# Maxima of two heads as 64-row products side by side, their unread result in PSUM, and the dense branch's output kept in the keys' room

## The chip, the cores and the metric

The kernel runs on one core of a Trainium2 chip. A core has a matrix engine (TensorE, PE in the profile, its weight loads on a row of their own, PEld), a vector engine (VectorE, DVE), a scalar engine (ScalarE, ACT), a general engine (GpSimd, POOL) and a sync engine (SyncE, SP) which here issues all DMAs, in order, from one queue. Operands lie in SBUF (128 partitions), results of TensorE in PSUM (eight banks of 2 KB per partition), inputs, outputs and scratch in HBM. The metric is the device time of one execution in microseconds.

## The reference, cut to what matters

```python
def reference(A_x, A_wqkv, A_wo, B_x, B_w1, B_b1, B_w2, B_b2, gate_w):   # S 2048, D 512, H 32, Dh 16, W 256, F 1792
    x = A_x
    g = sigmoid((x * gate_w).sum(-1, keepdims=True))
    q, k, v = heads(x @ wqkv)                       # 32 heads of 16
    scores = einsum("bhqd,bhkd->bhqk", q, k) * Dh ** -0.5
    scores = where(0 <= q_idx - k_idx < 256, scores, -1e9)
    a = heads_joined(softmax(scores) @ v) @ wo
    b = gelu(x @ w1 + b1) @ w2 + b2                 # dense branch, tanh form
    return g * a + (1 - g) * b
```

All is float32. Every query sees itself and the 255 positions before it.

## The kernel before, in words

**Precision.** Each float32 operand of a dense product is split into a high part rounded to TensorE's fast 32-bit format and the rest; `mm3` (L88 to L92) adds three products, so a dense step is three 128x512 matmuls of lines L90, L91 and L92.

**Two streams.** The generator `dense` yields dense work in such steps: `qkv` (projections, tiles `qk`, `v`), `mlp` (tiles `u`, then `y`, in two halves of the hidden width; `TURNS` gives the order of half and chunk of 512 rows), then `final` (tiles `a`, the output projection and the mix with the gate). Beside it runs attention, in units of one group of four heads (`g_`) and one block of 128 rows: 8 groups of 16 blocks, 128 units. A unit has four iterations; each does, in the order of `ORDER`, one maxima product (`att_max`, tile `sm`, L394), one scores product (`att_exp`, tile `st`, L435) for a unit eight units earlier (`LEAD`), and a filling of dense steps. The maxima are needed first because the row maximum is subtracted inside the scores product.

**Maxima.** `att_max` multiplies queries by keys, 128 queries against up to 384 keys, over 96 contraction rows: `qs[0:96]` and `ks[0:96]` hold the high and low parts of the queries and keys of two heads (of a pair `pr`); the two heads `s` of a pair share the rows, told apart by the columns of `ks` (`of_head`), where the other head's rows hold zeros. VectorE then adds the mask and takes the row maximum (L399), and writes the masked scores, which nobody reads, to a bfloat16 tile `jm` in SBUF. Line L399 is there twice: the pass over the scores, and a read of the accumulator into `M`. `sm` has three PSUM banks.

**Rows.** After four blocks `att_rows` negates and transposes the maxima, and GpSimd writes them to `qs[96:104]` (L419). `ks[96:104]` holds ones at the own head (`own`).

**Scores and values.** The scores product goes over all 128 rows; ScalarE exponentiates into `pt` (L450), GpSimd cuts the mask's triangles (L441, L444). Every fourth unit `att_pvs` multiplies `pt` by the values: matmuls of 64 rows by 32 columns with an explicit position in the array (`tile_position=(r, 32 * i)`, L476), eight positions, the two row halves into two PSUM banks (`pv_st`, `pv_sm`). All other matmuls take the array whole. These float32 products stand in the trace as two matmuls each.

**Loads of a chunk.** `att_load` fetches for a group and a chunk of 512 rows the keys (`load_k`) and the queries (L372, L373) from HBM scratch, one chunk per four units.

**The end.** Dense results of the two halves go to HBM (`YA`, `YB`); `final` reads back `YB` (`load_y`, L681), scales it by 1 - g on ScalarE (`scale_y`, L687, in place) and adds it (L716). Attention's results pass through HBM for the division (`att_norm`: `ND`, `RD`, `OT`) and come back in `load_o` (L561, tiles `or`, `ot`).

**What sets the order.** The order on each engine is written out by a small planner: `tick` advances a clock by the planned time of TensorE's work, `after(ns, ...)` puts the work of other engines on a list at a time of that clock, and each engine's queue gets its instructions in that order. `need` forces listed work forward. `GELU` holds the delays of the six steps of the activation function.

Of the kernel before, what the change touches and what calls it, by code (L numbers as in the profile page):

```python
# [18 lines left out]
T = 512  # L19
# [13 lines left out]
def gated_mix(ctx: ExitStack, tc: tile.TileContext, x, wqkv, wo, w1, b1, w2, b2, gate_w, out):  # L33
# [11 lines left out]
    def f32(ap):  # L45
        return ap.bitcast(F32)
# [3 lines left out]


    SQ = [dr.tile([H, 16, 2, T], F32, name=f"SQ{t}") for t in range(NT)]
    SK = dr.tile([H, 16, 2, S], F32, name="SK")
    SV = [dr.tile([T, H, 17], F32, name=f"SV{t}") for t in range(NT)]
    XT = [dr.tile([NC, 128, 2, T], F32, name=f"XT{t}") for t in range(NT)]
# [22 lines left out]
    for k in (0, 1):  # L78
        nc.gpsimd.affine_select(out=own[96:104], in_=own[96:104], pattern=[[-2, 4]], compare_op=ALU.not_equal,
                                fill=1.0, base=-k, channel_multiplier=1)  # L80
    nms = cp.tile([128, RB, 32], F32R, name="nm")
    nc.gpsimd.memset(f32(nms), 0.0)
    vbuf = cp.tile([128, 2, NB * 68 + 16], F32, name="vbuf")
# [76 lines left out]
    def load_now(key):  # L160
        load_raw(key)
        after(LAND, split, key, nc.vector)

# [184 lines left out]
    def load_k(g_, c, prs):  # L348


        need(("qk", c, NC + g_ // 2))
        for pr in range(prs.start, prs.stop):
            for s in range(2):
                src = SK[4 * g_ + 2 * pr + s]
                for r, n, part in ((32 * s, 32, src.rearrange("d u c -> (d u) c")), (64 + 16 * s, 16, src[:, 0])):
                    v = f32(ks[r:r + n, pr])
                    k0, m = (c * T, NB) if s == 0 else (c * T - 64, NB) if c else (64, NB - 1)
                    to = v[:, 2 * k0 + 64:2 * k0 + 64 + 256 * m] if s else v[:, 2 * k0:2 * k0 + 256 * m]
                    to = to.rearrange("r (n x) -> r n x", x=256)
                    to = to[:, :, 0:128] if s else to[:, :, 64:192]  # L360
                    nc.sync.dma_start(to, part[:, k0:k0 + 128 * m].rearrange("r (n x) -> r n x", x=128))
                    if s and c == 0:
                        nc.sync.dma_start(v[:, 0:64], part[:, 0:64])
                    if s and c == NT - 1:
                        nc.sync.dma_start(v[:, 2 * S - 64:2 * S], part[:, S - 64:S])

    def att_load(g_, c, q_only=False):
        need(("qk", c, g_ // 2))
        if not q_only:
            load_k(g_, c, slice(0, 2))  # L370
        src, to = SQ[c][4 * g_:4 * g_ + 4], f32(qs[:, :, c * T:(c + 1) * T])
        nc.sync.dma_start(to[0:64], src.rearrange("(a s) d u c -> (s d u) a c", a=2))  # L372
        nc.sync.dma_start(to[64:96], src[:, :, 1].rearrange("(a s) d c -> (s d) a c", a=2))  # L373

    def att_load_v(g_, c):
        need(*[("v", c, b) for b in range(NB)])
# [8 lines left out]
    def att_max(g_, b, i):  # L385

        if b % RB == 0 and (g_, b // RB) not in Ms:
            Ms[g_, b // RB] = sb.tile([128, RB, 4], F32, tag="M", bufs=2, name=f"M{g_}_{b}")
        M = Ms[g_, b // RB]
        k0 = max(b - 2, 0) * 128  # L390
        w = (b + 1) * 128 - k0
        pr, s = divmod(i, 2)
        p = ps.tile([128, 384], F32, tag="sm", bufs=3, name=f"sm{g_}_{b}_{i}")
        nc.tensor.matmul(p[:, :w], qs[0:96, pr, b * 128:(b + 1) * 128], of_head(ks[0:96, pr, 2 * k0:2 * (k0 + w)], s),  # L394
                         start=True, stop=True)
        junk = sb.tile([128, 384], BF16, tag="jm", bufs=1, name=f"jm{g_}_{b}_{i}")

        def red():
            nc.vector.tensor_tensor_reduce(junk[:, :w], p[:, :w], mask[:, 384 - w:384], 1.0, -3e38,  # L399
                                           ALU.add, ALU.max, M[:, b % RB, i:i + 1])  # L400
            done.add(("max", g_, b, i))
        tick(w / 2.4 + 13)
        after(100, red)

    def att_rows(g_, rb):
# [198 lines left out]
    def ya_load(k):  # L604
# [7 lines left out]
        else:  # L612
            need(("y", 0, t, b))
            nc.sync.dma_start(ya, YA[t][slice(b * 128, (b + 1) * 128)])

    def mlp(n):
        half, t = TURNS[n]
        if n == 0:
# [24 lines left out]
        def y_start(b):  # L643
            if n + 1 == len(TURNS) and b == 2:
                load_o(0)
            if n + 1 == len(TURNS) and b == 3:
                load_y(0)
            ps_[b] = ps.tile([128, D], F32, tag="d", bufs=2, name=f"y{t}_{half}{b}")

        def y_end(b):  # L650
            ts = slice(b * 128, (b + 1) * 128)
            y = sb.tile([128, D], F32, tag="sq", bufs=2, name=f"yo{t}_{half}{b}")
            nc.vector.scalar_tensor_tensor(y, ps_[b], 0.5, yas.pop(n * NB + b), op0=ALU.mult, op1=ALU.add)
            ya_load(n * NB + b + 2)
            nc.sync.dma_start((YA, YB)[half][t][ts], y)
            done.add(("y", half, t, b))


# [12 lines left out]
            if i == HF - 1:  # L671
                after(100, y_end, b)

    ybs = {}

    def load_y(t):

        need(*[("y", 1, t, b) for b in range(NB)])
        for i in range(NB // 2):
            v = f32(sb.tile([128, 2, T], F32R, tag="w", bufs=14, name=f"yb{t}_{i}"))  # L680
            nc.sync.dma_start(v, YB[t].rearrange("(i j p) f -> i p j f", j=2, p=128)[i])  # L681
            for j in range(2):
                ybs[t * NB + 2 * i + j] = v[:, j]

    def scale_y(nb):

        nc.scalar.activation(ybs[nb], ybs[nb], AF.Copy, scale=g1[:, nb:nb + 1])  # L687
        done.add(("yb", nb))

    def final(t):  # L690
        ot = xts["o", t]
        if t < NT - 1:
            load_o(t + 1, range(NC) if t < NT - 2 else range(NC - 1))
        for i in ((1, 2), (3,), (), ())[t]:
            load_y(i)
        for b in range(NB):
            ts = slice(b * 128, (b + 1) * 128)
            nb = t * NB + b
            if t == NT - 2 and b == 2:
                load_o(t + 1, range(NC - 1, NC))  # L700
            after(YLAND if nb == 0 else 0, scale_y, nb)
            a = sb.tile([128, 2, 320], F32, tag="pt", bufs=PTS, name=f"ao{nb}")
            a = a.rearrange("p a b -> p (a b)")[:, 0:D]
            n = LASTN if nb == NT * NB - 1 else 1
            for k in range(n):
                cs = slice(k * D // n, (k + 1) * D // n)
# [6 lines left out]

                def ev(p=p, nb=nb, a=a, cs=cs):
                    need(("yb", nb))
                    nc.vector.scalar_tensor_tensor(a[:, cs], p, g[:, nb:nb + 1], ybs[nb][:, cs],  # L716
                                                   op0=ALU.mult, op1=ALU.add)
                    nc.sync.dma_start(out[nb * 128:(nb + 1) * 128, cs], a[:, cs])
                after(100, ev)
# [35 lines left out]
    for u in range(-LEAD, NU):  # L755
# [26 lines left out]
MM3 = 3 * 227  # L782
LPOS = 0
LASTN = 2
YLAND = 3200
WARM = (7, 3)
RB = 4
NKB = S // 128
# [37 lines left out]
```

## Time and profile before

| | us |
| --- | --- |
| median of three runs | 776.58 (775.4 to 778.53) |
| the profiled execution | 779.54 |
| its span, first to last instruction | 777.6 |
| PE busy | 751.4 |
| DVE busy | 533.4 |
| ACT busy | 432.8 |
| POOL busy | 384.9 |

The mean granted TensorE clock was 0.993. A matmul's duration in the profile includes its way through the array, and its end is modelled; how long a matmul holds the array is read from the distance of two starts. A timeline row gives start, duration, engine, line, operation, tiles, shapes and, in brackets, the idle time before it. A "x2" at the end of such a row merges two instructions.

### The profile page before, as it was taken

The page shows a single profiled execution, that of the slowest core. Times are in us where ns is not written, and L with a number is a line of the kernel's source. Part 1 is how long each engine was busy: PE and PEld are TensorE (multiplying, and loading weights), DVE is VectorE, ACT ScalarE, POOL GpSimd, SP SyncE. Part 2 cuts the span into 40 slices and gives each one's busy share as a digit, 9 for nine tenths or more (in the row PEclk, how much of TensorE's full clock was granted, in tenths as well). Part 3 has the DMA queues.
Part 4 walks back from the last instruction along what each step waited for, and adds up shares of the span by engine and source line. Part 5 has one row for each costly group of instructions (what it writes and reads, how often), then busy time and mean ns, then how long its engine had stood idle before and what let it go on. Part 6 is the DMA issues. An engine that isn't in the chain of part 4 may idle for free.

```text
span 777.6 us, 18427 instructions
## 1 busy us (share of the span) xinstructions
PE 751.4 (97%) x6102; PEld 626.0 (81%) x6102; DVE 533.4 (69%) x1548; ACT 432.8 (56%) x945; POOL 384.9 (50%) x1125
## 2 busy tenths in 40 slices
PE   8999999989999999999999999999999999999978
PEld 5888888867888888788878877888888788878757
DVE  4532323889679868876997798679778867974433
ACT  4434433367468547754874676458548744875341
POOL 2200000028666765775676677657756774786000
PEclk9999999999999999999999999999999999999989
DMA  9986857755643665674436756642765563355772
GB/s 284 368 299 199 312 194 223 238 186 174 172 105 80 205 186 135 179 196 121 101 108 189 193 141 208 192 114 66 214 190 151 161 180 103 87 160 172 261 246 107
DMA packets 137680, 139.91 MB, mean 180 GB/s; under 512 B 53360, under 2 KB 88688, under 8 KB 137584
## 3 DMA queue, kind: packets, MB, share of 16 engines
q1 hardware_dynamic: 137584, 138.73, 59.8%
q8 instruction: 48, 0.79, 0.4%
q14 instruction: 48, 0.39, 0.2%
HBM read 83.63 MB, written 55.05 MB: 178 GB/s over the span
## 4 chain that ended last, share of the span: by engine, by line
PE 81%; DVE 8%; DMA 4%; issue 3%; ACT 2%; SPq 1%; DVEq 0%; ACTq 0%
PE sm L394 10%; PE st L435 8%; PE y L90 7%; PE y L91 6%; PE y L92 6%; PE u L90 5%; PE u L91 5%; PE u L92 5%; PE pv_st L476 4%; PE qk L92 4%; PE qk L90 4%; PE qk L91 4%; DVE jm L399 4%; PE pv_sm L476 4%; PE v L92 2%
## 5 line engine op out<-in xcount | busy, mean ns | idle before, releaser
L399 DVE CUSTOM_DVE_ANT_0 jm<-sm,mask 128x384 bf16<-128x384 f32 (+2 forms) x512 | 269.7, 527 | 67.7 <-PE sm L394 39.2
L450 ACT ACTIVATE pt<-st 128x320 f32<-128x320 f32 (+4 forms) x512 | 206.1, 421 | 134.1 <-PE st L435 127.1
L441 POOL TENSOR_SCALAR_AFFINE_SELECT pt<-pt 64x128 f32<-64x128 f32 x512 | 175.7, 343 | 187.4 <-ACT pt L450 167.5
L394 PE MATMUL sm<-ks,qs 96*128 96x384 f32 (+2 forms) x512 | 172.0, 339 | 10.2 <-DVE M L399 8.3
L435 PE MATMUL st<-qs,ks 128*128 128x320 f32 (+4 forms) x512 | 155.5, 306 | 0.7 <-ACT pt L450 0.7
L444 POOL TENSOR_SCALAR_AFFINE_SELECT pt<-pt 64x128 f32<-64x128 f32 x448 | 155.4, 347 | 0.0
L394 PEld LDWEIGHTS sm<-ks,qs 96*128 96x128 f32 x512 | 96.5, 188 | 43.1 <-DVE M L399 20.3
L435 PEld LDWEIGHTS st<-qs,ks 128*128 128x128 f32 x512 | 97.6, 191 | 18.2 <-ACT pt L450 1.1
L90 PE MATMUL y<-w,h 128*128 128x512 f32 x224 | 90.2, 403 | 0.0
L91 PE MATMUL y<-w,h 128*128 128x512 f32 x224 | 88.4, 395 | 0.0
L92 PE MATMUL y<-w,h 128*128 128x512 f32 x224 | 87.6, 391 | 0.0
L419 POOL CAST qs<-tt 8x256 fp32r<-8x256 f32 x128 | 61.5, 481 | 47.0 <-PE u L92 38.6
L90 PE MATMUL u<-mx,w 128*128 128x512 f32 x196 | 80.4, 410 | 0.0
L91 PE MATMUL u<-mx,w 128*128 128x512 f32 x196 | 77.3, 394 | 0.0
L92 PE MATMUL u<-mx,w 128*128 128x512 f32 x196 | 76.8, 392 | 0.0
L476 PE MATMUL pv_st<-pt,vbuf 64*32 64x320 f32 (+4 forms) x1408 | 73.5, 347 | 0.0
L476 PE MATMUL pv_sm<-pt,vbuf 64*32 64x320 f32 (+4 forms) x1408 | 73.0, 346 | 0.0
L476 PEld LDWEIGHTS pv_st<-pt,vbuf 64*32 64x32 f32 x1408 | 56.4, 106 | 4.7
L476 PEld LDWEIGHTS pv_sm<-pt,vbuf 64*32 64x32 f32 x1408 | 53.9, 106 | 7.5 <-issue 2.1
L251 DVE TENSOR_TENSOR qke<-qk,qke 128x512 fp32r<-128x512 f32 x32 | 22.1, 690 | 48.9 <-ACT qke L248 38.4
L248 ACT ACTIVATE qke<-qk 128x512 fp32r<-128x512 f32 x32 | 19.1, 598 | 55.8 <-PE qk L92 36.9
L92 PEld LDWEIGHTS y<-w,h 128*128 128x128 f32 x224 | 42.1, 188 | 9.8
(123 smaller groups left out, 1316.7 us busy)
## 6 DMA issues: line engine op xcount, KB each, us to landing
mx<-XT SPq DMA_DIRECT2D x24, 512.0 KB
SQ<-qke SPq DMA_DIRECT2D x16, 512.0 KB
SK<-qke SPq DMA_DIRECT2D x16, 512.0 KB
qs<-SQ SPq DMA_DIRECT2D x32, 256.0 KB
ND<-nd SPq DMA_DIRECT2D x32, 256.0 KB
ks<-SK SPq DMA_DIRECT2D x112, 64.0 KB
raw_w<-in_B_w_dram SPq DMA_DIRECT2D x28, 256.0 KB
SV<-vx SPq DMA_DIRECT2D x16, 272.0 KB
```

The source lines that it names most:

```text
L90: nc.tensor.matmul(p, lh, rh, start=first, stop=False)
L91: nc.tensor.matmul(p, lh, rl, start=False, stop=False)
L92: nc.tensor.matmul(p, ll, rh, start=False, stop=last)
L251: nc.vector.tensor_sub(e[:, 1 - h], p, f32(e[:, h]))
L394: nc.tensor.matmul(p[:, :w], qs[0:96, pr, b * 128:(b + 1) * 128], of_head(ks[0:96, pr, 2 * k0:2 * (k0 + w)], s), start=True, stop=True)
L399: nc.vector.tensor_tensor_reduce(junk[:, :w], p[:, :w], mask[:, 384 - w:384], 1.0, -3e38, ALU.add, ALU.max, M[:, b % RB, i:i + 1])
L419: nc.gpsimd.tensor_copy(dst, tt[32 * i:32 * i + 8].unsqueeze(1).broadcast_to([8, 2, RB, 32]))
L435: nc.tensor.matmul(p[:, :w], ks[:, pr, 2 * k0:2 * k0 + 128], qs[:, pr, k0:k0 + w], start=True, stop=True)
L441: nc.gpsimd.affine_select(out=v[:, :, 0:64], in_=v[:, :, 0:64], pattern=[[0, 2], [1, 64]], compare_op=ALU.is_ge, fill=0.0, base=0, channel ...
L444: nc.gpsimd.affine_select(out=v[:, :, W:W + 64], in_=v[:, :, W:W + 64], pattern=[[0, 2], [-1, 64]], compare_op=ALU.is_ge, fill=0.0, base=- ...
L450: nc.scalar.activation(pt[:, pr, :w], p[:, :w], AF.Exp, scale=SCALE)
L476: nc.tensor.matmul(pv[r // 64][32 * i:32 * i + 32, q - c * T:e - c * T], vs(i, r), rhs(r), start=start, stop=last, skip_group_check=True, ...
```

## The change

Contraction rows of the two heads of a pair no longer overlap: head 0 takes rows 0 to 55 and head 1 rows 64 to 119 (a gap of 8 rows in each), so the maxima product of a head has 56 rows and a position in a half of the array's rows. The two of a pair are issued one behind the other, in iterations 0 and 2 of a unit, where before each iteration had one. Rows 96 to 103, which receive the negated maxima later, now lie within head 1's rows; they are set to zero by a DMA from a zero tensor in HBM (`ZQ`) with each load of queries, and the two query DMAs of a chunk become four.

VectorE's pass writes its unread result over the scores in PSUM. The planner counts half the time for a maxima product, and the delays in `GELU` are reduced by 7 to 9%.

In the dense branch, `YB` of the first three chunks is loaded during the last group of heads, into the room of keys that are done with; the last chunk's results stay in SBUF and are not written to `YB`. `scale_y` writes to the output tile instead of in place, and its delay `YLAND` is gone.

```diff
+    ZQ = dr.tile([8, 2, T], F32, name="ZQ")
...
+    zero = sb.tile([128, 2, T], F32, tag="h", bufs=8, name="zero")
+    nc.gpsimd.memset(zero[0:8], 0.0)
+    nc.sync.dma_start(ZQ, zero[0:8])
...
@@ load_k
-                for r, n, part in ((32 * s, 32, src.rearrange("d u c -> (d u) c")), (64 + 16 * s, 16, src[:, 0])):
+                for r, n, part in ((64 * s, 32, src.rearrange("d u c -> (d u) c")), (64 * s + 40, 16, src[:, 0])):
...
@@ att_load
-        nc.sync.dma_start(to[0:64], src.rearrange("(a s) d u c -> (s d u) a c", a=2))
-        nc.sync.dma_start(to[64:96], src[:, :, 1].rearrange("(a s) d c -> (s d) a c", a=2))
+        nc.sync.dma_start(to[96:104], ZQ)
+        for s in range(2):
+            r = 64 * s
+            nc.sync.dma_start(to[r:r + 32], src.rearrange("(a s) d u c -> s (d u) a c", s=2)[s])
+            nc.sync.dma_start(to[r + 40:r + 56], src[:, :, 1].rearrange("(a s) d c -> s d a c", s=2)[s])
...
@@ att_max
-        nc.tensor.matmul(p[:, :w], qs[0:96, pr, b * 128:(b + 1) * 128], of_head(ks[0:96, pr, 2 * k0:2 * (k0 + w)], s),
-                         start=True, stop=True)
-        junk = sb.tile([128, 384], BF16, tag="jm", bufs=1, name=f"jm{g_}_{b}_{i}")
-
+        rows = slice(64 * s, 64 * s + 56)
+        nc.tensor.matmul(p[:, :w], qs[rows, pr, b * 128:(b + 1) * 128], of_head(ks[rows, pr, 2 * k0:2 * (k0 + w)], s),
+                         start=True, stop=True, tile_position=(64 * s, 0))
         def red():
-            nc.vector.tensor_tensor_reduce(junk[:, :w], p[:, :w], mask[:, 384 - w:384], 1.0, -3e38,
+            nc.vector.tensor_tensor_reduce(p[:, :w], p[:, :w], mask[:, 384 - w:384], 1.0, -3e38,
                                            ALU.add, ALU.max, M[:, b % RB, i:i + 1])
             done.add(("max", g_, b, i))
-        tick(w / 2.4 + 13)
+        tick((w / 2.4 + 13) / 2)
...
@@ mlp
-            if n + 1 == len(TURNS) and b == 3:
-                load_y(0)
...
-            y = sb.tile([128, D], F32, tag="sq", bufs=2, name=f"yo{t}_{half}{b}")
+            if n + 1 < len(TURNS) or b >= 2:
+                y = sb.tile([128, D], F32, tag="sq", bufs=2, name=f"yo{t}_{half}{b}")
+            else:
+                if b == 0:
+                    ybs["w"] = sb.tile([128, 2, T], F32, tag="w", bufs=14, name="yo")
+                y = ybs["w"][:, b]
...
-            nc.sync.dma_start((YA, YB)[half][t][ts], y)
+            if n + 1 < len(TURNS):
+                nc.sync.dma_start((YA, YB)[half][t][ts], y)
+            else:
+                ybs[t * NB + b] = y
...
@@ load_y
-            v = f32(sb.tile([128, 2, T], F32R, tag="w", bufs=14, name=f"yb{t}_{i}"))
+            v = f32(ks[:, i, 2 * t * T:2 * (t + 1) * T]).rearrange("p (j f) -> p j f", j=2)
...
@@ scale_y
-        nc.scalar.activation(ybs[nb], ybs[nb], AF.Copy, scale=g1[:, nb:nb + 1])
+        nc.scalar.activation(a, ybs[nb], AF.Copy, scale=g1[:, nb:nb + 1])
...
@@ final
-        for i in ((1, 2), (3,), (), ())[t]:
-            load_y(i)
...
-            after(YLAND if nb == 0 else 0, scale_y, nb)
...
+            after(0, scale_y, nb, a)
...
-                    nc.vector.scalar_tensor_tensor(a[:, cs], p, g[:, nb:nb + 1], ybs[nb][:, cs],
+                    nc.vector.scalar_tensor_tensor(a[:, cs], p, g[:, nb:nb + 1], a[:, cs],
...
@@ main loop
-                if op == "m" and m < NU:
-                    att_max(gm, bm, i ^ XOR)
+                if op == "m" and m < NU and i % 2 == 0:
+                    att_max(gm, bm, i), att_max(gm, bm, i + 1)
...
+        if u >= NU - NKB + NB and u % NB == 1:
+            load_y((u % NKB) // NB - 1)
...
-YLAND = 3200
-GELU = (700, 1500, 3600, 4600, 6000, 7000)
+GELU = (650, 1400, 3300, 4200, 5400, 6400)
-XOR = 1
```

On TensorE, one unit in the middle of the program (block 11 of a group for the maxima, block 3 of the same stretch for the scores). Before:

```order
L394 MATMUL sm_11_1_6601<-ks,qs 128x384
L435 MATMUL st_3_0_6606<-qs,ks 128x320
L90 MATMUL u_11_6549<-mx_4323,w_11_5573 128x512
L91 MATMUL u_11_6549<-mx_4323,w_11_5573 128x512
L92 MATMUL u_11_6549<-mx_4323,w_11_5573 128x512
L394 MATMUL sm_11_0_6615<-ks,qs 128x384
L435 MATMUL st_3_1_6618<-qs,ks 128x320
```

With the change (L403 is the maxima product, L442 the scores product, L94 to L96 are `mm3`):

```order
L403 MATMUL sm_11_0_6363<-ks,qs 128x384
L403 MATMUL sm_11_1_6365<-ks,qs 128x384
L442 MATMUL st_3_0_6368<-qs,ks 128x320
L94 MATMUL u_11_6314<-mx_4182,w_11_5394 128x512
L95 MATMUL u_11_6314<-mx_4182,w_11_5394 128x512
L96 MATMUL u_11_6314<-mx_4182,w_11_5394 128x512
L442 MATMUL st_3_1_6378<-qs,ks 128x320
```

The second maxima product has moved ahead of a scores product and a dense step, to stand behind its partner; the number of matmuls is the same.

On SP's queue, the stretch that carries the last normalisations at the end of the program (`ND`, `RD`, `OT` are attention's way through HBM, `or` its way back, `yb` the dense branch's). Before:

```order
L681 DMA yb_1_11007<-YB_124 128x2x512
L681 DMA yb_0_11009<-YB_125 128x2x512
L681 DMA yb_1_11011<-YB_125 128x2x512
L532 DMA OT_84<-num_3_10835 128x512
L655 DMA YB_126<-yo_13_10945 128x512
L522 DMA RD_3_114<-den_3_10884 128x32
L561 DMA or_0_10997<-OT_84 128x512
L561 DMA or_1_10999<-OT_84 128x512
L561 DMA or_2_11001<-OT_84 128x512
L561 DMA or_3_11003<-OT_84 128x512
L527 DMA num_3_11045<-ND_3_98 128x1x512
L527 DMA rb_3_11047<-RD_3_114 128x1x512
```

With the change (the same chunk's steps):

```order
L568 DMA or_0_10582<-OT_85 128x512
L568 DMA or_1_10584<-OT_85 128x512
L539 DMA OT_85<-num_3_10424 128x512
L529 DMA RD_3_115<-den_3_10470 128x32
L568 DMA or_2_10586<-OT_85 128x512
L568 DMA or_3_10588<-OT_85 128x512
L534 DMA num_3_10622<-ND_3_99 128x1x512
L534 DMA rb_3_10624<-RD_3_115 128x1x512
```

The three `yb` loads ahead of the store to `OT` and the store to `YB` behind it are gone from this place; six loads of `YB` now stand between the query and value loads of the last group, further up the queue.

More of the change, by code (lines that the diff above doesn't have):

```diff
@@ L614, in ya_load @@
             nc.sync.dma_start(ya, YA[t][slice(b * 128, (b + 1) * 128)])
+    ybs = {}
     def mlp(n):
@@ L672, in mlp @@
                 after(100, y_end, b)
-    ybs = {}
     def load_y(t):
@@ L683, in load_y, with scale_y @@
                 ybs[t * NB + 2 * i + j] = v[:, j]
-    def scale_y(nb):
-        nc.scalar.activation(ybs[nb], ybs[nb], AF.Copy, scale=g1[:, nb:nb + 1])
+    def scale_y(nb, a):
+        nc.scalar.activation(a, ybs[nb], AF.Copy, scale=g1[:, nb:nb + 1])
         done.add(("yb", nb))
```

## Prediction

> **What bounds the kernel now.** I read the page's sums and its chain first, then the busy times by stretch.
>
> ```profile
> span 777.6 us, 18427 instructions
> PE 751.4 (97%) x6102; PEld 626.0 (81%) x6102; DVE 533.4 (69%) x1548; ACT 432.8 (56%) x945; POOL 384.9 (50%) x1125
> ...
> PE 81%; DVE 8%; DMA 4%; issue 3%; ACT 2%; SPq 1%; DVEq 0%; ACTq 0%
> ```
> ```profile
> core 0: us, PE busy (x) PEld busy (x) DVE busy (x) ACT busy (x) POOL busy (x), PEclk, DMA share, GB/s
> 160.00:690.00 530.00, 517.89 (x4785) 434.70 (x4784) 427.82 (x1324) 335.02 (x748) 350.45 (x1020) 1.00 0.55 154
> ...
> 720.00:735.00 15.00, 13.31 (x59) 10.75 (x58) 6.75 (x10) 6.27 (x11) 0.00 (x0) 1.00 0.80 266
> 735.00:750.00 15.00, 9.31 (x41) 7.39 (x40) 5.78 (x10) 4.97 (x8) 0.00 (x0) 0.95 0.67 226
> 750.00:777.60 27.60, 24.30 (x108) 20.12 (x106) 9.31 (x14) 6.09 (x10) 0.00 (x0) 0.91 0.47 157
> ```
>
> TensorE holds 81% of the chain. From 160 to 690 us, where attention and dense work are interleaved, it is busy 517.9 of 530 us; VectorE, the next, 427.8 (81%). In that stretch, what lengthens a unit on TensorE lengthens the kernel nearly one for one. The end, after 720, is another matter: TensorE has holes there, and the clock drops after one of them (0.91).
>
> How long a maxima product holds TensorE is the distance of two starts. One step of the timeline, and the groups by shape:
>
> ```profile
> 400.40 0.39 PE L92 MATMUL y<-w,h 128*128 128x512 f32 x1
> 400.63 0.34 PE L394 MATMUL sm<-ks,qs 96*128 96x384 f32 x1
> 400.80 0.31 PE L435 MATMUL st<-qs,ks 128*128 128x320 f32 x1
> 400.95 0.40 PE L90 MATMUL y<-w,h 128*128 128x512 f32 x1
> ```
> ```profile
> L394 PE MATMUL sm<-ks,qs 96*128 96x384 f32 x448 | 155.7, 351 | 10.2 <-DVE M L399 8.3 <-DVE nd L498 1.4
> ...
> L394 PE MATMUL sm<-ks,qs 96*128 96x256 f32 x32 | 9.0, 282 | 0.0
> ...
> L394 PE MATMUL sm<-ks,qs 96*128 96x128 f32 x32 | 7.3, 227 | 0.0
> ```
>
> A dense matmul takes 0.23, a wide maxima product 0.17, a scores product 0.15. So a wide pair costs 0.34 today, and there are 224 wide pairs and 32 narrow ones. Weight loads cost nothing here, since each runs under the matmul before it.
>
> **The price of using the array in parts.** The trace has 32 batches of value products, which take the array in parts of 64 rows by 32 columns, and around each the array goes from whole to parts and back. On the way in, a scores product is followed by the first load of a part; on the way out, the last part by a dense step:
>
> ```profile
> 501.15 0.31 PE L435 MATMUL st<-qs,ks 128*128 128x320 f32 x1
> ...
> 501.38 0.10 PEld L476 LDWEIGHTS pv_sm<-pt,vbuf 64*32 64x32 f32 x1 [0.22 <-DVE M L399]
> ```
> ```profile
> 415.04 0.22 PE L476 MATMUL pv_sm<-pt,vbuf 64*32 64x64 f32 x1
> ...
> 415.20 0.19 PEld L90 LDWEIGHTS y<-w,h 128*128 128x128 f32 x1
> 415.21 0.50 PE L90 MATMUL y<-w,h 128*128 128x512 f32 x1
> 415.31 0.19 PEld L91 LDWEIGHTS y<-w,h 128*128 128x128 f32 x1
> ...
> 415.54 0.40 PE L91 MATMUL y<-w,h 128*128 128x512 f32 x1
> ```
>
> In: 0.23 from the scores product to the load, where it hands over after 0.15 otherwise: 0.08 lost. Out: the last part has 64 columns, about 0.03 of streaming (0.23 x 64 / 512), yet the load of `y` begins 0.16 after it: 0.13 lost. And that load is in the open: the next matmul comes 0.33 later instead of 0.23, 0.10 more. The load did not start under the matmul before it, as all loads of the whole array do. So a change of shape costs 0.08 to 0.13 of silence, plus an uncovered load of 0.10 for 128 columns.
>
> The parts themselves do run side by side:
>
> ```profile
> 413.82 0.43 PE L476 MATMUL pv_sm<-pt,vbuf 64*32 64x320 f32 x1
> 413.83 0.43 PE L476 MATMUL pv_st<-pt,vbuf 64*32 64x320 f32 x1
> ...
> 414.09 0.43 PE L476 MATMUL pv_sm<-pt,vbuf 64*32 64x320 f32 x1
> ```
>
> Neighbours start 0.01 apart, and the round of eight positions repeats after 0.27, where eight scores products of that width would need 1.2.
>
> The Trainium skill, "TensorEngine Tiling (Array Packing)", section "Key Properties", states that changing the tiling mode, not just the tile, drains TensorE, and lists 64x128 among the modes. That rule speaks against this change; it gives no duration. By it the pairs pay at both ends, and the trace agrees for 64x32 with 0.08 and 0.13. No run here shows 64x128.
>
> **The change part by part.**
>
> *Pairs.* Between dense steps or scores products, which take the whole array, each pair of 64x128 products now goes in and out of parts. New price of a wide pair: silence in 0.08, load in the open 0.10 (both loads at once, since neighbouring parts start 0.01 apart), one stream 0.17, the second's start 0.01, silence out 0.13, load of the following scores product 0.10: 0.59 against 0.34, so +0.25, times 224 = +56. Narrow pairs by the same steps with shorter streams: about +0.29 each, times 32 = +9. Together **+65**. Both ends of this price: if 64x128 switches for nothing, a pair costs 0.18 and the term is -0.16 x 224 - 2 (the narrow ones) = -38; if the two loads go one after the other, +0.10 x 256 = +26 on top. I take the middle one, because the nearest row, 32 batches alike, is a switch of shape between the same neighbours.
>
> *Waits of the maxima.* `sm` keeps three banks but is filled two at a time, so the second of a pair reuses the bank of the previous pair's first, half a unit back instead of three quarters. Today TensorE waits here:
>
> ```profile
> PEld sm L394 <- DVE M L399: 20.3, 39, 1.6
> ...
> PE sm L394 <- DVE M L399: 8.3, 16, 1.2
> ```
>
> The two PE rows tell of the same waits, 8 to 20 us. With a unit some 0.5 us longer and the same VectorE work (427.8 over about 590 us, 73%), these shrink: **-8** (0 to -20). Behind a waiting product stand the scores product and dense step; both have their slack in the same 0.5.
>
> *Result over the scores.* No row shows VectorE writing PSUM. Nearest are the present pass and a sum of two inputs that reads PSUM and writes SBUF in float32:
>
> ```profile
> L399 DVE CUSTOM_DVE_ANT_0 jm<-sm,mask 128x384 bf16<-128x384 f32 x448 | 247.2, 552 | 55.0 <-PE sm L394 29.8 <-PE st L435 0.3
> ...
> L653 DVE SCALAR_TENSOR_TENSOR yo<-y,ya 128x512 f32<-128x512 f32 x32 | 21.9, 686 | 7.6 <-PE y L92 7.6
> ```
>
> 552 for 384 columns and 686 for 512 lie on one line of 1.05 ns a column, so the type costs nothing; the place I bound by 0.1 us either way, +-51 us of VectorE time in 512 passes. At 73 to 81% load it is hidden: 0.
>
> *Loads of a chunk.* Three more DMAs for each of 32 chunks, on SP's queue:
>
> ```profile
> L372 SPq DMA_DIRECT2D qs<-SQ x32: 579/582/759, 112.6 to 659.1; - x32
> ```
>
> At 0.58 each the last query rows are issued 1.7 us later. A chunk is loaded four units (over 16 us) ahead, which covers it: 0; uncovered it would be 32 x 1.7 = 56.
>
> *The end.* Loads of `YB` leave the last stretch. What they delayed, from the chain:
>
> ```profile
> 718.27 8.43 DMA OT<-num
> ...
> 728.47 5.44 DMA ND<-nd
> ...
> 736.39 6.55 DMA or<-OT
> ...
> 749.36 0.76 PE a L90
> 750.12 0.43 PE a L91
> ...
> 755.52 0.23 PE a L92
> ```
> ```profile
> 716.41 1.43 SPq L681 DMA_DIRECT2D yb<-YB  x3
> 718.27 0.33 SPq L532 DMA_DIRECT2D OT<-num  x1
> ```
> ```profile
> PE a L90 <- DVE ao L716: 7.4, 2, 5.7
> ```
>
> Three `yb` loads are issued just ahead of the 8.43 us store, and SP stands behind that store until the `or` loads can go. Without 1.5 MB in front (5.9 us at the 266 GB/s of that stretch), the store lands some 4 us earlier, and the steps behind it about as much again. TensorE's two holes (7.4 together) and the slow matmuls behind the larger one (14 matmuls at 0.43 instead of 0.23, 2.8) are worth at most 10: I take **-8** (0 to -10). The writes of `scale_y` to another tile, the `GELU` delays and the zero tensor at the start move nothing on this path: 0.
>
> Sum against the profiled span: 777.6 + 65 - 8 - 8 = 826.6. The median of the runs lies 1 us below that span, so **826**; its own range 800 to 855.
>
> **The rivals.** A: *a switch of rows alone is free.* The value batches split columns as well, and their price may belong to that. For it: products of 96 of 128 rows fit in without a gap. Against: the uncovered load, which depends on nothing but the shape. The pair then costs 0.18: -38. But VectorE is then at 427.8 over about 490, 87%, and its waits grow; I put the 14 us in the middle of today's waits on top: +14. With -8 from the end: 777.6 - 32 - 1 = 745 (728 to 765); it decides from a switch cheaper than 0.08 at each end. If PSUM writes cost 0.1 us a pass, VectorE is at 97% and most of this is gone.
>
> The Trainium skill, "TensorE: Matmul & The Clock Gate", section "Step-by-step: what each phase is for", says that column tiling takes four or eight buses into the array and row tiling no extra one. By that, a switch of rows could be the cheap one, as in A; no row here shows it.
>
> B: *half of the price.* Either the silence is paid and the loads are covered (0.39 a pair, +13 in all), or the reverse (0.38, +10). With -8 from the end and -4 from waits: about 776, 768 to 790, no difference to speak of.
>
> C: *the halves don't overlap.* The pair keeps two streams and pays the switch: 0.17 more for each, +44 on the forecast, 870. The start distance of 0.01 between opposite row halves speaks against it.
>
> **How the numbers follow.** Forecast 0.58, A 0.30, B 0.09, C 0.03. A change under 0.5% (3.9 us) is none for this measurement, whose three runs span 0.4%. B splits into 0.03 faster, 0.05 the same, 0.01 slower. Faster: 0.30 + 0.03 = 0.33; same 0.05; slower: 0.58 + 0.03 + 0.01 = 0.62. The range reaches from the middle of A to the forecast's upper end: 742 to 850. It leaves out half of A or a bit less, and C.
>
> **What would show it.** The distances of starts around a pair: from the dense matmul to the first maxima load 0.31 or more instead of under it, scores product 0.5 or more behind the pair's start. If the loads of the pair lie under the dense matmul and the scores product follows 0.18 behind, A holds. VectorE's share between 160 and the end of attention near 73%, or near 87%. The pass over the scores near 552. At the end: no `PE a L90` wait of 5.7, and a clock of 1.00 after 720; if the hole stays, the term -8 was wrong. The forecast fails as a whole if the unit's 256 pairs show no uncovered load.

## The result

The changed kernel takes **826.2 us** (median of four, 824.8 to 829.8), against 777.6 for the kernel before: a ratio of 1.063, 95% interval 1.060 to 1.067. It is 6.3% slower, and the forecast was 826. The next sections show that this agreement is partly luck: the largest term was right in kind and slightly too large, and four smaller ones that were missed or mis-sized cancel.

The page of the changed kernel, and its busy times in the stretch in which attention and dense work are interleaved:

```profile
span 825.9 us, 18090 instructions
PE 805.1 (97%) x6102; PEld 576.4 (70%) x6102; DVE 537.4 (65%) x1548; ACT 433.2 (52%) x945; POOL 375.9 (46%) x1126
...
PE 91%; DMA 4%; DVE 2%; SPq 1%; ACT 1%; issue 1%; POOL 0%; ACTq 0%; DVEq 0%
```
```profile
160.00:690.00 530.00, 519.55 (x4418) 354.78 (x4418) 392.99 (x1210) 301.04 (x672) 310.12 (x932) 0.99 0.51 145
```

TensorE is as full as before, 519.6 of 530 us, but gets through fewer matmuls in that time (4418 instead of 4785). VectorE, with the same number of instructions in the whole program, has fallen from 81% to 74% of this stretch; it now waits for TensorE. TensorE's share of the chain has grown from 81 to 91%.

One unit of the changed kernel in the timeline, the matmuls and the weight loads (in two fences, since they are two rows of the profile; "x2" is the pair, which the view merges):

```profile
433.14 0.40 PE L95 MATMUL y<-w,h 128*128 128x512 f32 x1
433.37 0.40 PE L96 MATMUL y<-w,h 128*128 128x512 f32 x1
433.70 0.44 PE L403 MATMUL sm<-ks,qs 56*128 56x384 f32 x2
434.06 0.42 PE L442 MATMUL st<-qs,ks 128*128 128x320 f32 x1
434.32 0.39 PE L94 MATMUL y<-w,h 128*128 128x512 f32 x1
```
```profile
433.14 0.19 PEld L96 LDWEIGHTS y<-w,h 128*128 128x128 f32 x1
433.69 0.19 PEld L403 LDWEIGHTS sm<-ks,qs 56*128 56x128 f32 x2 [0.37 <-DVE M L406]
434.06 0.19 PEld L442 LDWEIGHTS st<-qs,ks 128*128 128x128 f32 x1 [0.18 <-issue]
434.17 0.19 PEld L94 LDWEIGHTS y<-w,h 128*128 128x128 f32 x1
```

Read the load of `y` at 433.14: it starts with the matmul before its own, under cover. The pair's load at 433.69 does not: the last dense matmul started at 433.37 and would hand over at 433.60, and only 0.09 later does the load begin. The row's bracket names VectorE as what the load waited for, but that is not what holds it. Of the 217 pairs behind a dense matmul, 213 have their load 0.315 to 0.326 after that matmul's start, whatever the row names and also where it names none (`issue`); the other four stand at long holes or a few us behind them. A wait for VectorE would vary.

The load of the scores product after the pair stands in the open too, and that matmul's row begins together with its load (0.42 long instead of 0.31). From the last dense matmul to the next one it is 434.32 - 433.37 = 0.95. Without a pair it would be a dense matmul and a scores product, 0.23 + 0.15 = 0.38. So a pair now costs 0.57, where it cost 0.34 before: +0.23. For 256 pairs, the 32 narrow ones taken alike, that is 59 us.

TensorE's waits in the changed kernel (us in total, times, longest):

```profile
PE sm L403 <- DMA qs<-SQ: 6.8, 4, 3.0
PE a L94 <- DVE ao L727: 4.7, 1, 4.7
PE sm L403 <- DVE M L406: 3.6, 5, 1.3
```

The first of them did not exist before. The second is the hole at the end, 5.7 at its longest before. These rows list matmuls; a wait of the weight loads has rows of its own (PEld), and the two tell in part of the same time.

### The profile page after: what moved, and what is told of

It reads as the page before. It is cut to its first block, busy times and chain, and to the rows that moved or that the text cites. A ratio compares the mean times of both kernels' runs of the same rounds, so it can differ in the third digit from the quotient of the medians.

```text
span 825.9 us, 18090 instructions
## 1 busy us (share of the span) xinstructions
PE 805.1 (97%) x6102; PEld 576.4 (70%) x6102; DVE 537.4 (65%) x1548; ACT 433.2 (52%) x945; POOL 375.9 (46%) x1126
## 4 chain that ended last, share of the span: by engine, by line
PE 91%; DMA 4%; DVE 2%; SPq 1%; ACT 1%; issue 1%; POOL 0%; ACTq 0%; DVEq 0%
PE st L442 14%; PE sm L403 11%; PE y L94 7%; PE y L95 6%; PE y L96 6%; PE u L94 6%; PE u L96 6%; PE u L95 6%; PE pv_st L483 5%; PE qk L94 4%; PE pv_sm L483 4%; PE qk L96 4%; PE qk L95 4%; PE v L96 2%; PE v L94 2%; PE v L95 2%
## 5 line engine op out<-in xcount | busy, mean ns | idle before, releaser
L406 DVE CUSTOM_DVE_ANT_0 sm<-sm,mask 128x384 f32<-128x384 f32 (+2 forms) x512 | 263.2, 553 | 99.2 <-PE sm L403 98.3
L457 ACT ACTIVATE pt<-st 128x320 f32<-128x320 f32 (+4 forms) x512 | 211.2, 424 | 202.2 <-PE st L442 195.4
L448 POOL TENSOR_SCALAR_AFFINE_SELECT pt<-pt 64x128 f32<-64x128 f32 x512 | 174.8, 341 | 246.7 <-ACT pt L457 230.0
L442 PE MATMUL st<-qs,ks 128*128 128x320 f32 (+4 forms) x512 | 175.0, 354 | 0.0
L451 POOL TENSOR_SCALAR_AFFINE_SELECT pt<-pt 64x128 f32<-64x128 f32 x448 | 145.8, 326 | 0.0
L442 PEld LDWEIGHTS st<-qs,ks 128*128 128x128 f32 x512 | 93.7, 188 | 52.7 <-issue 29.7
L403 PE MATMUL sm<-ks,qs 56*128 56x384 f32 (+2 forms) x512 | 114.8, 428 | 10.5 <-DMA qs<-SQ 6.8
L403 PEld LDWEIGHTS sm<-ks,qs 56*128 56x128 f32 x512 | 50.2, 184 | 102.9 <-issue 48.0
L94 PE MATMUL y<-w,h 128*128 128x512 f32 x224 | 90.9, 406 | 0.0
L95 PE MATMUL y<-w,h 128*128 128x512 f32 x224 | 89.3, 399 | 0.0
L96 PE MATMUL y<-w,h 128*128 128x512 f32 x224 | 89.2, 398 | 0.0
L94 PE MATMUL u<-mx,w 128*128 128x512 f32 x196 | 80.2, 409 | 0.0
L96 PE MATMUL u<-mx,w 128*128 128x512 f32 x196 | 77.4, 395 | 0.0
L406 DVE DVE_READ_ACCUMULATOR2_ANT M<- 128x1 f32 x512 | 71.9, 140 | 0.0
L505 DVE TENSOR_TENSOR nd<-nd,pv_sm 128x512 f32<-128x512 f32 x32 | 21.9, 683 | 43.8 <-ACT nd L502 43.8
```

The lines of the kernel that those rows point to most:

```text
L94: nc.tensor.matmul(p, lh, rh, start=first, stop=False)
L95: nc.tensor.matmul(p, lh, rl, start=False, stop=False)
L96: nc.tensor.matmul(p, ll, rh, start=False, stop=last)
L403: nc.tensor.matmul(p[:, :w], qs[rows, pr, b * 128:(b + 1) * 128], of_head(ks[rows, pr, 2 * k0:2 * (k0 + w)], s), start=True, stop=True, ti ...
L406: nc.vector.tensor_tensor_reduce(p[:, :w], p[:, :w], mask[:, 384 - w:384], 1.0, -3e38, ALU.add, ALU.max, M[:, b % RB, i:i + 1])
L442: nc.tensor.matmul(p[:, :w], ks[:, pr, 2 * k0:2 * k0 + 128], qs[:, pr, k0:k0 + w], start=True, stop=True)
```

## The experiments

Two questions were open: is the price really that of the change of shape, and what do the other parts of the change do that are carried along with it?

### The pair on the whole array

Everything of the change, but each product runs over all 128 rows; the other head's keys are zeros in these columns, so the result is the same.

```diff
-        rows = slice(64 * s, 64 * s + 56)
+        rows = slice(0, 128)
...
-                         start=True, stop=True, tile_position=(64 * s, 0))
+                         start=True, stop=True)
```

> The changed kernel with one edit: the maxima products take all 128 contraction rows and the whole array, still two behind each other, everything else as changed. Switch theory (each pair goes into halves and back, 0.10 of silence and 0.10 of uncovered weight load at each end): the 256 pairs give back about 58 us and VectorE's waits take some 8 back, 776 us (768 to 785). Rival (the loss lies in the chunk loads, in writing PSUM or in the new order, and halves of rows are nearly free): 815 us or more.

788.7 us (785.7 to 794.4), ratio 1.015 (1.010 to 1.020). The halves account for 826.2 - 788.7 = **37.5 us**. In this kernel the loads of the pair lie under the dense matmul before it, and that of the scores product under the pair:

```profile
434.41 0.39 PE L96 MATMUL y<-w,h 128*128 128x512 f32 x1
434.63 0.51 PE L403 MATMUL sm<-ks,qs 128*128 128x384 f32 x2
434.99 0.31 PE L442 MATMUL st<-qs,ks 128*128 128x320 f32 x1
435.13 0.39 PE L94 MATMUL y<-w,h 128*128 128x512 f32 x1
```
```profile
434.41 0.42 PEld L403 LDWEIGHTS sm<-ks,qs 128*128 128x128 f32 x2
434.81 0.19 PEld L442 LDWEIGHTS st<-qs,ks 128*128 128x128 f32 x1
434.99 0.19 PEld L94 LDWEIGHTS y<-w,h 128*128 128x128 f32 x1
```

From dense to dense 0.72 and, less 0.38, 0.34 for a pair. The time is above the 768 to 785 of the switch theory and far below the rival's 815: other parts of the change cost time as well. And the 59 us of the pairs are not given back in full, because TensorE now waits longer than it did with the slower unit:

```profile
PE sm L403 <- DVE M L406: 10.6, 16, 1.8
PE sm L403 <- DMA qs<-SQ: 5.7, 1, 5.7
...
PE sm L403 <- DMA vbuf<-SV: 3.7, 1, 3.7
```

Together 20.0 against 10.4 at the same place in the changed kernel. The rest is in shorter delays. Added up over all 256 pairs, from the start of the matmul before a pair to that of the second one behind it, the two traces differ by 38.9 us. Had every pair taken the time of undelayed pairs with the same neighbours (their lower quartile), the difference would be 57.0; what goes beyond that time is 33.7 us on the whole array and 15.5 in halves. So 18 of the 21.5 between 59 and 37.5 are delays that the slower unit does not have.

### One product at a time in halves

The halves stay, but each iteration has one product, with whole-array work on both sides of it: twice the changes of shape for the same products.

```diff
-                if op == "m" and m < NU and i % 2 == 0:
-                    att_max(gm, bm, i), att_max(gm, bm, i + 1)
+                if op == "m" and m < NU:
+                    att_max(gm, bm, i)
```

> The changed kernel with one edit: one maxima product in each iteration, as before the change, but each still in its half of the rows, so that 512 products stand alone instead of 256 pairs. Switch theory: price by the switch, so every single product pays 0.10 silence, 0.10 load, 0.10 silence, 0.10 load on its stream of 0.17, 0.39 more than a whole-array product, times 512 = 200 on about 770: 965 us (930 to 1000). Rival (price by the product, because 56 rows in a half stream slowly): the same 512 products, 826 us, within 10.

946.7 us in the one run, inside the 930 to 1000 of the switch theory and 158 more than the pair on the whole array. The rival (826) has fallen: the price hangs on how often the shape changes, not on the products. It is less than the 200 forecast, and no `PE sm` row is left among TensorE's waits in this kernel, so part of the price falls on time that was waited before.

```profile
434.19 0.39 PE L96 MATMUL u<-mx,w 128*128 128x512 f32 x1
434.51 0.44 PE L403 MATMUL sm<-ks,qs 56*128 56x384 f32 x1
434.87 0.41 PE L442 MATMUL st<-qs,ks 128*128 128x320 f32 x1
435.12 0.39 PE L94 MATMUL u<-mx,w 128*128 128x512 f32 x1
```

From dense to dense 0.93 for one head, against 0.95 for two above. The load behind a dense matmul begins 0.315 to 0.326 after its start here too, in all 437 cases. So the second product of a pair is almost free, the halves do run side by side, and the whole 0.57 is the way into halves and out again, with one stream in it.

### The dense branch's edit alone

The kernel before with `YB` loaded into the room of the keys, the last results kept in SBUF, and `scale_y` to the output tile, and nothing else of the diff.

> The kernel before with the dense branch's edit alone (loads of its results in the keys' room during the last group, last chunk kept in SBUF, scaling into the output tile). Prediction's term: 8 less, 769. By the changed kernel's trace, where a hole of 4.9 us and the slow clock behind it are still there: 4 less, 773. Rival (the transfers were hidden anyway): no difference, 777.

772.3 us (771.3 to 775.3), ratio 0.993 (0.991 to 0.995): **-5.7**. The hole at the end has shrunk:

```profile
PE a L90 <- DVE ao L721: 2.4, 1, 2.4
```

It was 7.4 in two waits before.

### The unread result in PSUM alone

```diff
-        junk = sb.tile([128, 384], BF16, tag="jm", bufs=1, name=f"jm{g_}_{b}_{i}")
...
-            nc.vector.tensor_tensor_reduce(junk[:, :w], p[:, :w], mask[:, 384 - w:384], 1.0, -3e38,
+            nc.vector.tensor_tensor_reduce(p[:, :w], p[:, :w], mask[:, 384 - w:384], 1.0, -3e38,
```

> The kernel before with one edit: the unread result of the maxima's pass goes over the scores in PSUM. Prediction's term: hidden, 776 to 779. Rival (the read of the accumulator behind each pass takes 140 ns in the changed kernel instead of 82, 512 x 58 ns = 30 us more on VectorE, which the shorter units of the kernel before do not hide whole): 5 to 12 more, 782 to 789.

766.2 us (765.2 to 767.1), ratio 0.985 (0.983 to 0.987): **-11.8**, though no theory had a gain here. The instructions have become slower, not faster (groups of this kernel, mean ns behind the busy time):

```profile
L398 DVE CUSTOM_DVE_ANT_0 sm<-sm,mask 128x384 f32<-128x384 f32 (+2 forms) x512 | 267.2, 543 | 47.9 <-PE sm L394 46.1 <-PE st L434 0.4
...
L398 DVE DVE_READ_ACCUMULATOR2_ANT M<- 128x1 f32 x512 | 70.9, 138 | 0.0
```
```profile
L399 DVE CUSTOM_DVE_ANT_0 jm<-sm,mask 128x384 bf16<-128x384 f32 (+2 forms) x512 | 269.7, 527 | 67.7 <-PE sm L394 39.2 <-PE st L435 0.3
...
L399 DVE DVE_READ_ACCUMULATOR2_ANT M<- 128x1 f32 x512 | 42.0, 82 | 0.0
```

The second fence is the kernel before. Compare the last column, the idle time ahead of the pass. Before, 67.7 us, of which the two releasers named account for 39.5: 28 us of idle time have no name. With the result in PSUM it is 47.9, and 46.5 have one. The view names a releaser only for idle times above 0.15 us, so the nameless 28 us are many short ones. VectorE's own order shows where they stood, before:

```profile
420.49 0.56 DVE L399 CUSTOM_DVE_ANT_0 jm<-sm,mask 128x384 bf16<-128x384 f32 x1 [0.57 <-PE sm L394]
420.98 0.08 DVE L399 DVE_READ_ACCUMULATOR2_ANT M<- 128x1 f32 x1
420.98 0.69 DVE L531 TENSOR_TENSOR num<-num,rb 128x512 f32<-128x512 f32 x1
...
423.24 0.56 DVE L399 CUSTOM_DVE_ANT_0 jm<-sm,mask 128x384 bf16<-128x384 f32 x1
423.73 0.08 DVE L399 DVE_READ_ACCUMULATOR2_ANT M<- 128x1 f32 x1
423.95 0.56 DVE L399 CUSTOM_DVE_ANT_0 jm<-sm,mask 128x384 bf16<-128x384 f32 x1
```

Other work behind a pass starts 0.49 after it (420.49 and 420.98). A second pass behind a pass starts 0.71 after it (423.24 and 423.95). The new idea: `jm` has one buffer, so a pass may not write before the one ahead of it has ended. The rows of line L399 in the view by source show an extra instruction on VectorE's queue in the kernel before that the other kernel does not have:

```profile
L399 DVEq EVENT_SEMAPHORE  x480: 21/21/21, 133.3 to 690.1; - x160
```

### The same result in SBUF, with three buffers

```diff
-        junk = sb.tile([128, 384], BF16, tag="jm", bufs=1, name=f"jm{g_}_{b}_{i}")
+        junk = sb.tile([128, 384], BF16, tag="jm", bufs=3, name=f"jm{g_}_{b}_{i}")
```

(and the same count where the tag is used for the warm-up's operand).

> The kernel before, with three buffers in turn for the unread result of the maxima pass instead of one, still 16-bit in SBUF. In the trace of before no pass follows another in less than 0.58 us (5% point; median 0.71), though other work follows a pass after 0.48; with the result in PSUM a pass follows a pass after 0.48 too. One theory, the buffer: the single buffer made each pass wait until the one ahead of it had ended. Then three buffers give the whole gain of the result in PSUM: 766 (764 to 769), and consecutive passes 0.48 apart where nothing else is late. Rival, the place: a write to SBUF is what is slow. Then this stays at 777 (775 to 779.5), and consecutive passes stay 0.58 and more apart.

764.8 us (764.2 to 766.9), ratio 0.984 (0.982 to 0.985). It was the single buffer; the place brings no gain. Passes now follow each other as other work does, and the accumulator is read in 0.08 as before:

```profile
416.66 0.56 DVE L399 CUSTOM_DVE_ANT_0 jm<-sm,mask 128x384 bf16<-128x384 f32 x1 [0.40 <-PE sm L394]
417.14 0.08 DVE L399 DVE_READ_ACCUMULATOR2_ANT M<- 128x1 f32 x1
417.14 0.55 DVE L399 CUSTOM_DVE_ANT_0 jm<-sm,mask 128x384 bf16<-128x384 f32 x1
```

In the kernel before, none of the 243 passes that stand directly behind a wide one starts less than 0.64 behind it; here 127 of them start within 0.58. TensorE's waits for the pass, 20.3 us before, fell to:

```profile
PEld sm L394 <- DVE M L399: 11.3, 18, 1.6
```

### The two good edits together

> The kernel before with the two edits that were faster by themselves: the unread result over the scores in PSUM (-11.8) and the dense branch's output kept out of the round trip (-5.7). They act at different places, the passes between 160 and 700 and the tail behind the last value product. If they add: 760 (757 to 763). Rival, both only shift the start of the same hole in the tail: 766 (764 to 768).

**760.9 us** (759.7 to 762.1), ratio 0.978 (0.976 to 0.980): 11.8 and 5.3 add, as forecast. This is 2.2% faster than the kernel before, and 65 us faster than the change as a whole. It serves as the base of the next runs.

### Where the other 28 us come from

788.7, the pair on the whole array, is 28 more than this base. Four parts of the change lie between them: the order in pairs, the new rows with five loads of queries a chunk, the planner's half time for a product, and the delays in `GELU`. First the order alone, on the base:

> The two edits of the run before and, added, the order of the change alone: both maxima products of a pair of heads one behind the other on every second turn, on the rows 0 to 95 and with the loads of before. The halves' price is 37.5 (826.2 less 788.7, the change on the whole array); what lies between 788.7 and the two good edits is some 28 and is not explained. One theory, the order: pairs bunch VectorE's passes, and TensorE waits for it at the second product. Then 784 to 791, with some 28 of TensorE's waits at the maxima for VectorE. Rival, the loads: the order costs nothing, 758 to 764, with less than 16 of such waits. Between: a split.

767.5 us (764.9 to 769.6): **+6.6**. It lies between the two forecasts, nearer to the one without a cost; the weight loads' waits for VectorE at the maxima rose from 12.0 to 18.7 us. Then the change on the whole array without the pairs:

```diff
-                if op == "m" and m < NU and i % 2 == 0:
-                    att_max(gm, bm, i), att_max(gm, bm, i + 1)
+                if op == "m" and m < NU:
+                    att_max(gm, bm, i ^ 1)
```

> The change on the whole array, with the order of before: one maxima product a turn, on all 128 rows, with the five query loads of each chunk, the zero rows, and the shorter GELU distances of the change. By the order theory the 28 are gone: 760 to 768, of which up to 6 are TensorE's waits for the query loads. By the loads theory it stays at 784 to 791.

785.4 us (784.9 to 787.7): **+24.5** on the base. So the order is not the main cause, and something that this kernel shares with the change is. Its waits at the maxima, and three stretches around the longest of them (duration, then busy time with number of instructions of PE, PEld, DVE, ACT and POOL, then the granted clock):

```profile
PE sm L403 <- DMA vbuf<-SV: 5.3, 1, 5.3
PE sm L403 <- DVE M L406: 4.6, 11, 1.1
...
PE sm L403 <- DMA qs<-SQ: 3.9, 1, 3.9
```
```profile
200.00:206.00 6.00, 0.69 (x4) 0.28 (x3) 0.59 (x4) 0.30 (x1) 1.23 (x5) 0.75 0.42 99
206.00:210.00 4.00, 4.00 (x12) 3.23 (x12) 1.41 (x8) 0.87 (x2) 1.01 (x4) 0.52 0.96 180
210.00:215.00 5.00, 5.00 (x111) 4.34 (x111) 1.71 (x8) 1.84 (x5) 2.39 (x8) 1.00 0.64 152
```

TensorE stands for 5.3 us, waiting for loads. Then it works for some 4 us at a granted clock of 0.52, which costs about 2 us more (an estimate: 4 x 0.48). Which of the three remaining parts brings these holes? Each alone, on the base:

```diff
-        nc.sync.dma_start(to[0:64], src.rearrange("(a s) d u c -> (s d u) a c", a=2))
-        nc.sync.dma_start(to[64:96], src[:, :, 1].rearrange("(a s) d c -> (s d) a c", a=2))
+        for s in range(2):
+            nc.sync.dma_start(to[32 * s:32 * s + 32], src.rearrange("(a s) d u c -> s (d u) a c", s=2)[s])
+            nc.sync.dma_start(to[64 + 16 * s:80 + 16 * s], src[:, :, 1].rearrange("(a s) d c -> s d a c", s=2)[s])
```

> The kernel before with the two good edits (760.95), and each chunk's two query loads of 64 and 32 rows split into four of 32 and 16 rows, as the change has them; same bytes, same rows. The change on the whole array with the order of before is 24 longer than 760.95, and shows four holes of 5.3, 3.9, 2.0 and 1.9 us on TensorE at the maxima, three of them ended by a load, each with a granted clock near 0.5 for some 4 us behind it. One theory, the number of loads: each further one makes SyncE's queue later. Then 770 to 782, with holes at the maxima that end with a query load. Rival, the zero rows: their load alone is what is late; then this stays at 759 to 763. Second rival, the shorter GELU distances: 759 to 763 too.

767.8 us (766.6 to 769.2): **+6.8**, less than the theory asked for, with one new wait:

```profile
PE sm L395 <- DMA qs<-SQ: 3.2, 1, 3.2
```

The expectation counted four holes at the maxima; the one of 1.9 us stands at a value product, ends with VectorE, and the granted clock behind it is 1.00. Behind the 3.2 us here the clock is 0.57 for 4 us, so this one stall costs about 5 us, an estimate. Ahead of the late query load, SP's queue itself waits, for transfers issued earlier to land (`rb<-RD` 1.7 us, `mx<-XT` 1.5). Such waits stand in the base's queue too; why they meet a query load here and not there was not tested.

Only the load of zeros added (`ZQ`, as in the change):

> The same two edits (760.95), and only the load of zeros into rows 96 to 103 added, ahead of each chunk's two query loads; nothing reads these zeros in this kernel. It waits for whatever last used these rows. By the theory of the zero rows 775 to 785; by the number of loads some 2 to 7 longer (763 to 768); by GELU no change.

761.5 us (760.6 to 762.5): +0.5, nothing. Only the delays of `GELU`:

> The same two edits (760.95), and only the six distances of the dense branch's steps of the change (650, 1400, 3300, 4200, 5400, 6400 in place of 700, 1500, 3600, 4600, 6000, 7000). By the theory of GELU, the dense stages ask VectorE and ScalarE for more than they can give in that time: 775 to 785. By both theories of the loads: 758 to 764.

763.1 us (760.7 to 763.6): +2.1, hardly more than the runs differ. These three, if they add, make 9.4 of 24.5. What was left was the planner's half time, or an effect of the loads together. The last run gives back the planner's times to the kernel of 785.4:

```diff
-        tick((w / 2.4 + 13) / 2)
+        tick(w / 2.4 + 13)
...
-GELU = (650, 1400, 3300, 4200, 5400, 6400)
+GELU = (700, 1500, 3600, 4600, 6000, 7000)
```

> The change on the whole array with the order of before (785.40), and the planner's times of before: a maxima product counts in full, and GELU's distances are 700 to 7000. What is left of the change against 760.95 is the place of the rows (all 128, heads at 0 and 64) and the five query loads of a chunk. One theory, the plan: half the time for a product that still takes its whole time puts the other engines' work and the loads at wrong places, and that makes the 15 to 17 which the split loads (+6.8), the zeros (+0.5) and GELU (+2.1) leave of the 24.4. Then 766 to 771. Rival, the loads together: five on one queue do what four and one do not. Then 780 to 787, with the holes at the maxima that end with a load.

772.0 us (771.0 to 775.1): **-13.4** by the planner's times, 1 us above that theory's range, and well under the rival's. The hole at 205 us is gone, the one that ends with a query load stays:

```profile
PE sm L403 <- DVE M L406: 9.8, 16, 1.7
PE sm L403 <- DMA qs<-SQ: 4.0, 1, 4.0
```
```profile
200.00:206.00 6.00, 6.00 (x112) 5.13 (x115) 3.39 (x16) 2.29 (x6) 4.40 (x15) 1.00 0.74 142
```

What rows and loads cost by themselves is thus 772.0 - 760.9 = 11.1, of which the split explains 6.8. The other 4 may lie in TensorE's waits at the maxima for VectorE, 9.8 us in place of 5.6 in the base; their reason is not shown. On the whole array, half the time in the plan and the shorter delays cost 13 together. With 2.1 for the delays, some 11 would be the half time's; it was not run by itself. Whether it is wrong in halves too, where a pair holds TensorE for 0.57 and not 0.17, was not run.

The bill, each step between two kernels that were run (778.1 is the kernel before in the later rounds):

| step | us |
| --- | --- |
| kernel before | 778.1 |
| one buffer's wait gone (result in PSUM) | -11.8 |
| dense branch's edit | -5.3 |
| new rows, five query loads a chunk | +11.1 |
| the planner's half time and GELU's delays | +13.4 |
| order in pairs | +3.3 |
| products in halves | +37.5 |
| changed kernel (sum 826.3) | 826.2 |

A step has its price in its place: the order in pairs costs 6.6 on the base and 3.3 here, where it is the difference of 788.7 (785.7 to 794.4) and 785.4, no more than the runs differ.

## Why the prediction was right, and where it was not

**The pairs, +65.** The mechanism is shown, and only the silence out is a remainder and not read from a row. Predicted for a wide pair: 0.59 (silence in 0.08, load 0.10, stream 0.17, silence out 0.13, load 0.10); measured 0.57. The silence in was 0.09 in the row above, the load of the scores product in the open took 0.26 - 0.15 = 0.11, so the silence out was about 0.10. The load of a pair begins 0.32 after the dense matmul's start, where the prediction asked for 0.31 or more. The price taken from batches of 64x32 parts holds for 64x128 as well, and thereby rival A (a switch of rows is free, 745) is refuted by the two runs in halves; so is B, since silence and load are both paid, and C, since one product costs what two cost. By that the rule of the Trainium skill, "TensorEngine Tiling (Array Packing)", section "Key Properties", holds here for row tiling too: the trace agrees, with 0.09 and 0.10 of silence. "What would show it" asked for a scores product 0.5 behind the pair's start; its matmul's row begins 0.36 after the pair's, since the row of a matmul with an open load begins with the load. The 0.5 was right only for the stream.

**The waits of the maxima, -8.** The sign was right, the size too small. In place of 65 - 8 = 57, the halves and pairs together cost 37.5 + 3.3 = 41. VectorE's share was forecast at 73% and is 74%. The slower unit hides more of the loads and of VectorE than a term made from the waits of the kernel before could show: on the whole array, the changed kernel has 33.7 us of delays around its pairs, in halves 15.5.

**The result over the scores, 0.** Wrong by 11.8, and not for a reason that the step had looked at. It priced the place (0.1 us either way) and took the time as hidden. The place did cost 0.02 for the pass and 0.06 for the accumulator, and that was hidden. But the edit also took away the single buffer `jm`, and with it a wait of each pass for the one ahead. A sign of it was there to read: 28 us of idle time without a releaser in the group of the pass, which the prediction quoted in its shape of 384 columns (55.0, of which 30.1 have a name).

**The loads of a chunk, 0.** Wrong by 6.8 for the split of the query loads by itself, and by 11.1 with the new rows and the zeros. The step priced the time of issuing, 1.7 us a chunk, against a lead of over 16 us. It did not look at what the queue waits for between its issues, nor at the clock behind a stall. The result showed the lateness at once, in 6.8 us of waits for `qs<-SQ`.

**GELU and the half time.** GELU's delays were put at 0, and alone they are 2.1. The planner's half time had no step at all; with the delays it is 13.4 on the whole array, and its price in halves is not known. This is the second term that was missed.

**The end, -8.** By itself -5.7, and -5.3 on top of the other edit; inside the range of 0 to -10. The hole that was to go has only shrunk, to 2.4 alone and to 4.7 in the changed kernel, where the last matmul of the values starts at 770.7 and the program ends 55.2 later; before it was 58.1 (719.5 to 777.6). In the changed kernel that stretch is thus 2.9 shorter, and the term -8 was wrong there, as the prediction said it would be if the hole stayed.

So the sum agrees to 0.4 us because terms cancel: +57 forecast against +41 for halves and pairs, -8 against -5 for the end, 0 against -12 for the result, 0 against +24 for loads and plan. The sign rests on one term, and this one was found in a row of the kernel before.

## What to carry to other kernels

A matmul that uses part of TensorE's array between matmuls that use all of it pays its way in and out, here some 0.4 us for each visit, with one product in it or two side by side; gather several such matmuls behind one change of shape (here two), or leave the array whole. When a group's idle time exceeds what its releasers account for, look for a tile with a single buffer, even one that nobody reads: three buffers in place of one gave 1.6% here. And cost an edit by everything that it takes away, its buffer and its place in the plan too, not only by the operation that it names.

## What the runs showed of the hardware

- **TensorE's clock behind a hole.** After TensorE had stood for 5.3 us, its granted clock was 0.52 over the next 4 us, and 1.00 after that, in the rows above. This hole thus costs more than its length, by about 2 us. Not every hole does: in the same run the clock stayed at 1.00 behind the one of 1.9 us.
- **The accumulator's read.** A maxima pass that writes to PSUM has its accumulator read in 0.138 us, against 0.082 where it writes to SBUF; the pass itself takes 543 ns on the mean instead of 527.
- **Two loads at once.** The weight loads of the two halves stand in the trace as one row of 0.19 us for both, where the two of a pair on the whole array take 0.42; they run together, and so do the products behind them, whose starts are 0.003 us apart (median of 256 pairs).
